# Merged transposing transfers, rows of the summed tanh gradient by DMA, and a shifted last x gradient block in a joint-network training step

## The chip, the cores and the metric

The kernel runs on one core of a Trainium2 chip. The metric is the time of one execution on the device in microseconds (us); a run gives one time, and the median over runs is used. The profile is of one execution, recorded by the hardware profiler.

A core has a matrix engine (PE, with its weight loads in a row of their own, PEld), a vector engine (DVE), an activation engine (ACT), a general engine (POOL) and a sync engine (SP). Each works through its own instructions in order and waits for the others by semaphores. In this kernel SP issues transfers on queue q1 and POOL on queue q0. PE writes into PSUM accumulators, which DVE or ACT copy away.

## The reference

Forward part and gradient of a small joint network: two convolutions with stride 2 over x, a projection, a tanh over the sum of two projections, and an output product.

```python
B, T, D, K, U = 2, 16000, 256, 3, 8
h  = gelu(conv(x, w1))[:, ::2]        # K = 3 taps, 256 -> 256
f  = gelu(conv(h, w2))[:, ::2]        # [2, 4000, 256]
fe = f @ w_f
ge = g @ w_g                          # [2, 8, 256]
j  = tanh(fe[:, :, None, :] + ge[:, None, :, :])
out = j @ w_o                         # [2, 4000, 8, 256]
```

The kernel returns `out` and, for a given `grad_out` of the same shape, the gradients of x, w1, w2, g, w_f, w_g and w_o. All arrays are bfloat16; sums are kept in float32.

## The kernel before

The 4000 output positions of both batch rows are laid one after the other (with 16 columns between) and cut into 16 chunks of 512 columns (`CW`); the last is 336 wide. Features lie on the 128 partitions in two halves (`KT`), positions along the free axis. Products that sum over positions (the weight gradients) need the same data with positions on the partitions ("rows"), so much of the kernel is transposes: by PE through PSUM, or by transposing DMA transfers that SP issues.

The main loop (L829) runs over the chunks n. Within it four steps `up` handle two of the eight u each. A step (`joint_units`, L674) does this for its u: `gj` (L616) squares the tanh JT on ACT into JSQ, multiplies grad_out (GOT, features on partitions) with w_o on PE, and DVE forms NGZ; POOL sums NGZ over u into ACCN and, for the last u, into NGFE (`ngfe_acc`, L636): the summed tanh gradient. Then four blocks of `out` are computed (L694), copied by ACT (L696) and stored by POOL (L721), and the w_o gradient of the step before is accumulated (`gwo`, L725, matmul L733) from JR, the rows of JT, and GO, the rows of grad_out.

Between the units of a step `weave` (L746) sets filler units, 0.92 for each main unit, taken in a written order (`parts`, L833 to L842). For chunk n they are: the first convolution of chunk n+1 (`conv_units`, matmul L320) with the product d1 of chunk n-1 in it (`d1_units`, L424, reading NGFE; DVE writes GF at L426); the row transposes of chunk n-1 braided with the product d5 (`row_units`, `d5_units`, L447); the w_f gradient (`gwf_units`, L506, reading the rows FR of f and NR of NGFE); the w2 gradient (L524); rows of GH; the second convolution of chunk n+1 (L355); and `e_units` (L567): four x gradient blocks (matmul L584, copied by ACT at L587 into GX, stored by POOL at L241) with three w1 gradients (L597) between. After six of the eleven e units stands `fe_units` of chunk n+1 (L379), whose FE feeds the tanh (`tanh`, L390) of the next iteration.

SP issues the transposing transfers: XC, the four phases of x (`load_x`, L164, two chunks ahead, one phase per step); GOT, one per u, two steps ahead (`load_got`, L172); JR, one per u, from JT, a step ahead (`load_jr`, L662); FR, two per chunk (`load_fr`, L469); and the plain transfer GO, one per step (`load_go`, L198). The 512-column tile of 256 features that one of them moves is 256 KB (FR: 128 KB each). NR, the rows of NGFE, is made by PE: eight transposes (L460, in `transposes`) and one DVE copy (L462) at the head of `row_units`.

What sets the order: each tile comes from a pool of so many buffers (`xcp` 6, `gotp` 5, `jtp` 7, `jrp` 2, `frp` 1, `rowp` 6, `gxp` 2), and whoever writes a buffer waits until the last reader of its former content is done. A list scheduler orders the instructions of each engine from the program order and a cost model; the compiled order of each engine is fixed. The transfers issued by SP use eight completion semaphores in turn, so each waits for the eighth before it. The tail after the loop finishes chunk 15.

Of the kernel before, what the change touches and what calls it, by code (L numbers as in the profile page):

```python
# [22 lines left out]
P = 128  # L23
KT = 2
# [8 lines left out]
def kernel(  # L33
# [28 lines left out]
    xq = x.rearrange("b (q four) d -> b four q d", four=4)  # L62
# [39 lines left out]
    xcp = pool("xcp", 6)  # L102
# [10 lines left out]
    rowp = pool("rowp", 6)  # L113
    xrp = pool("xrp", 1)
    gxp = pool("gxp", 2)
    jtp = pool("jtp", 7)
    gotp = pool("gotp", 5)
# [38 lines left out]
    def load_x(n, phases=(0, 1, 3, 2)):  # L156
        W = geom(n)[1]
        for c in phases:
            t = xcp.tile([P, KT, CW + 16], BF16, name="XC")
            back = 16 if c == 3 else 0  # L160
            for lo, hi in gaps(n, back):
                nc.vector.memset(t[:, :, 16 + lo:16 + hi], 0.0)
            for b, q, col, w in segs(n, back):
                nc.sync.dma_start_transpose(out=t[:, :, 16 + col:16 + col + w], in_=xq[b, c, q:q + w, :])  # L164
            S[n]["X", c] = t

    def load_got(n, u):
        t = gotp.tile([P, KT, CW], BF16, name="GOT")
        for lo, hi in gaps(n):
            nc.vector.memset(t[:, :, lo:hi], 0.0)  # L170
        for b, q, col, w in segs(n):
            nc.sync.dma_start_transpose(out=t[:, :, col:col + w], in_=grad_out[b, q:q + w, u, :])  # L172
        S[n]["GOT", u] = t
# [216 lines left out]
    def tanh(n, u):  # L390
        c0, W = geom(n)
        JT = jtp.tile([P, KT, CW], BF16, name="JT")
        S[n]["JT", u] = JT
        for mt in range(KT):
            for b, lo, hi in spans(n):
                nc.scalar.activation(out=JT[:, mt, lo:hi], in_=S[n]["FE"][:, mt, lo:hi], func=ACT.Tanh,  # L396
                                     bias=GE[:, b, mt, u:u + 1], scale=1.0)
        if W % P:
            nc.gpsimd.memset(JT[:, :, W:W // P * P + P], 0.0)

# [62 lines left out]

    def load_fr(n):
        W = geom(n)[1]
        FR = frp.tile([P, KT, 4, P], BF16, name="FR")
        nb = len(blocks(W))
        for kt in range(KT):
            nc.sync.dma_start_transpose(out=FR[:, kt, 0:nb, :], in_=S[n]["FT"][:, kt, 0:nb * P])  # L469
        S[n]["FR"] = FR  # L470

    def row_units(n):
        c0, W = geom(n)
        st = S[n]
        HT, GF, FT, NG = st["HT"], st["GF"], st["FT"], st["NGFE"]
        bl = blocks(W)
        FR = st["FR"]
        t = rowp.tile([P, 8, P], BF16, name="rows")
        st["NR"] = t
        srcs = [(NG[:, kt, o:o + M], 2 * j + kt, M) for j, (o, M) in enumerate(bl) for kt in range(KT)]  # L480
        dsts = [(t[:M, 2 * j:2 * j + 2, :], M, 2 * j, 2 * j + 2) for j, (o, M) in enumerate(bl)]
        if W == CW:
            dsts = [(t[:], P, 0, 8)]
        transposes(srcs, dsts)
        yield
        st["HG"] = []
        s = nsets(n)
        for k, M in sets(n):
            t = rowp.tile([P, 8, P], BF16, name="rows")
            col = lambda off: slice(off + k, off + k + s * (M - 1) + 1, s)  # L490
            srcs = [(HT[:, par, kt, col(2)], 2 * par + kt, M) for par in range(2) for kt in range(KT)]
            srcs += [(GF[:, kt, col(2)], 4 + kt, M) for kt in range(KT)]
            if k == 0:
                srcs += [(HT[:, 1, kt, col(1)], 6 + kt, M) for kt in range(KT)]
            transposes(srcs, [(t[:M, 0:len(srcs)], M, 0, len(srcs))], nc.scalar.copy)
            st["HG"].append(t)
            yield

    def gwf_units(n):
        W = geom(n)[1]  # L500
        FR, t = S[n]["FR"], S[n]["NR"]
        bl = blocks(W)
        ps = ps_f32()
        for k, (o, M) in enumerate(bl):
            for dt in range(KT):
                nc.tensor.matmul(ps[:, dt * D:(dt + 1) * D], lhsT=FR[:M, dt, k, :],  # L506
                                 rhs=t[:M, 2 * k:2 * k + 2, :].rearrange("p k d -> p (k d)"),
                                 start=(k == 0 and dt == 0), stop=(k == len(bl) - 1 and dt == KT - 1))
        flush("F", ACCF[:], ps[:])
        first_flush["F"] = False  # L510
        yield
# [19 lines left out]
    def braid(rows, d5):  # L531
        for gen in (rows, d5, rows, d5, rows, d5, rows, rows, d5):
            yield next(gen, None)
# [118 lines left out]
    def load_jr(n, up):  # L652

        W = geom(n)[1]
        JR = jrp.tile([P, 2, KT, 4, P], BF16, name="JR")
        S[n]["JR", up] = JR
        if n == 0:
            return
        for j in range(2):
            JT = S[n]["JT", 2 * up + j]  # L660
            if W == CW:
                nc.sync.dma_start_transpose(out=JR[:, j].rearrange("p k a d -> p (k a) d"),  # L662
                                            in_=JT[:].rearrange("p k w -> p (k w)"))
            else:
                nb = len(blocks(W))
                for kt in range(KT):
                    nc.sync.dma_start_transpose(out=JR[:, j, kt, 0:nb, :], in_=JT[:, kt, 0:nb * P])
# [99 lines left out]
    idle = xcp.tile([P, KT, CW + 16], BF16, name="XC")  # L767
    nc.vector.memset(idle[:], 0.0)
# [4 lines left out]
    def warm(k):  # L773

        ps = ps_f32()
        for _ in range(k):
            tc.keep_in_program_order(nc.tensor.matmul(ps[:], lhsT=idle[:, 0, 0:P], rhs=idle[:, 0, 0:CW],
                                                      start=True, stop=True))
        yield
# [35 lines left out]
    for i in range(2):  # L815
        load_got(*order[i])
    load_go(*orderp[0])
    for i in range(2, 4):
        load_got(*order[i])
# [7 lines left out]

    for n in range(G):
# [5 lines left out]
        if back:  # L834
            d1, e, rows, ghr = d1_units(n - 1), e_units(n - 1), row_units(n - 1), ghr_units(n - 1)
            parts += [islice(conv, 2), islice(d1, 1), islice(conv, 1), d1, conv, braid(rows, d5_units(n - 1)),
# [3 lines left out]
            parts.append(e)  # L840
# [4 lines left out]
        for up in range(U // 2):  # L845
            step = n * (U // 2) + up
            for i in range(2):
                if 2 * step + 4 + i < len(order):
                    load_got(*order[2 * step + 4 + i])
# [21 lines left out]
            if n + 2 < G:  # L871
                load_x(n + 2, ((0, 1, 3, 2)[up],))
# [5 lines left out]
    for _ in chain(d1_units(n), alternate(row_units(n), d5_units(n)), gwf_units(n), gw2_units(n), ghr_units(n), e_units(n)):  # L878
        pass
# [24 lines left out]
    for b in range(B):  # L904
# [3 lines left out]
        gg_sb = gxp.tile([U, D], BF16, name="gg_sb")  # L908
        nc.scalar.activation(out=gg_sb[:], in_=gg[:U, 0:D], func=ACT.Copy, scale=-1.0)
        nc.sync.dma_start(out=out_4[b], in_=gg_sb[:])  # L910
# [3 lines left out]
        ngR = gxp.tile([U, KT, P], BF16, name="ngR")  # L914
        nc.vector.tensor_copy(out=ngR[:], in_=tr[:U, 0:KT, :])
# [37 lines left out]
```

## Time and profile before

Three runs took 847.09, 842.17 and 854.28 us, a median of 847.09.

| | |
|---|---|
| profiled execution | 845.37 us, its span 843.6 us |
| DVE, ACT, POOL busy | 73%, 81%, 47% |
| mean granted TensorE clock | 0.992 |
| moved by DMA | 187.21 MB, mean 222 GB/s |
| GOT, JR, XC, FR transfers | 136, 128, 68, 32 |
| GO transfers of 512 KB | 56, 5.2 us to landing |
| ACT waits for JR<-JT before a tanh | 8.1 us in 4 waits |

The page gives, for each engine, its busy time and its share of the span; queues with packets, MB and the time that their packets took as a share of sixteen engines' span; and the chain of work that ended last, followed back from the end. A timeline row reads: start, length, engine, line, operation, what it writes and reads, how many in a row, and in brackets the engine's idle time before it with what ended that. A "q" behind an engine's name is its sequencer: a transfer's row on SP is the time that its issue took there, not that of the transfer.

### The profile page before, as it was taken

To read this page: it belongs to the slowest core of one execution; us is meant where nothing else is said; L and a number is where in the kernel's file an instruction comes from. 1 tells how busy PE (TensorE), PEld (TensorE's weight loads), DVE (VectorE), ACT (ScalarE), POOL (GpSimd) and SP (SyncE) were. 2 spreads that over 40 slices of the span, in tenths; PEclk is the share of its full clock that TensorE was granted. 3 is DMA by queue.
4 is the path that set the end of the run, shared out by engine and by line. 5 is a ranking of instruction groups with operands and counts; after the bars stand their busy time and mean duration, and the time that the engine had idled before them with its cause. 6 is when DMAs were issued, how large, how long until landed. Compare 5 with 4: busy or idle time off the path is not lost.

```text
span 843.6 us, 17055 instructions
## 1 busy us (share of the span) xinstructions
PE 816.5 (97%) x6396; PEld 600.8 (71%) x6396; DVE 619.7 (73%) x1217; ACT 679.8 (81%) x1080; POOL 393.8 (47%) x423
## 2 busy tenths in 40 slices
PE   8979999999999999999989999999999999999997
PEld 4556777868777676777757767777776877878796
DVE  4996786877769677696856957769687776967744
ACT  3889997896978969699786886979879697987744
POOL 1145653443544434545465643454444454455661
PEclk9989999999999999999999999999999999999999
DMA  9978999999999999999999999999999999999964
GB/s 197 203 183 182 241 214 235 239 237 219 223 202 230 241 216 265 217 229 212 227 218 220 223 229 212 254 225 253 247 247 220 232 266 242 197 213 223 245 162 135
DMA packets 398515, 187.21 MB, mean 222 GB/s; under 512 B 346464, under 2 KB 382200, under 8 KB 398432
## 3 DMA queue, kind: packets, MB, share of 16 engines
q1 hardware_dynamic: 378112, 119.00, 78.9%
q0 software_dynamic: 20320, 67.12, 27.3%
q8 instruction: 50, 0.82, 0.4%
q14 instruction: 33, 0.27, 0.1%
HBM read 51.38 MB, written 50.34 MB: 121 GB/s over the span
## 4 chain that ended last, share of the span: by engine, by line
PE 71%; ACT 15%; DMA 6%; DVE 6%; issue 2%; ACTq 0%
PE GWO_ps L733 10%; PE ps L694 9%; PE ps L627 8%; PE ps L597 8%; PE ps L584 7%; DMA JR<-JT 6%; PE ps L524 5%; PE ps L320 5%; PE ps L355 4%; PE pst L460 4%; ACT JT L396 4%; PE ps L447 4%; ACT JSQ L621 2%; ACT OUT L696 2%; DVE NGZ L631 2%
## 5 line engine op out<-in xcount | busy, mean ns | idle before, releaser
L631 DVE SCALAR_TENSOR_TENSOR NGZ<-JSQ,ps 128x512 bf16<-128x512 bf16 (+3 forms) x272 | 168.3, 640 | 47.7 <-PE ps L627 44.4
L650 POOL TENSOR_TENSOR ACCN<-ACCN,NGZ 128x1024 f32<-128x1024 f32 (+1 forms) x80 | 168.6, 2107 | 70.8 <-DVE NGZ L631 69.7
L696 ACT CAST OUT<-ps 128x512 bf16<-128x512 f32 (+1 forms) x252 | 148.5, 600 | 53.3 <-PE ps L694 53.1
L396 ACT ACTIVATE JT<-FE,GE 128x512 bf16<-128x512 f32 (+3 forms) x272 | 182.2, 709 | 10.7 <-DMA JR<-JT 8.1
L733 PE MATMUL GWO_ps<-GO,JR 128*128 128x256 bf16 (+1 forms) x1008 | 150.8, 274 | 5.9 <-DMA JR<-JT 3.8
L621 ACT ACTIVATE JSQ<-JT 128x1024 bf16<-128x1024 bf16 (+1 forms) x128 | 135.8, 1064 | 25.5 <-DVE NGZ L631 24.8
L694 PE MATMUL ps<-WO,JT 128*128 128x256 bf16 (+1 forms) x1008 | 149.1, 274 | 2.2 <-ACT rows L462 1.4
L721 POOL DMA_DIRECT2D out_dram<-OUT x76 | 55.8, 734 | 182.8 <-ACT OUT L696 165.4
L627 PE MATMUL ps<-GOT,WOT 128*128 128x512 bf16 (+1 forms) x512 | 138.8, 376 | 1.2 <-ACT OUT L696 1.2
L733 PEld LDWEIGHTS <-JR 128*128 128x128 bf16 (+1 forms) x1008 | 97.0, 98 | 37.0 <-DMA JR<-JT 4.9
L694 PEld LDWEIGHTS <-JT 128*128 128x128 bf16 (+1 forms) x1008 | 98.5, 99 | 25.2 <-issue 4.8
L260 DVE SCALAR_TENSOR_TENSOR g_s<-g_sq,g_x 128x1024 bf16<-128x1024 bf16 (+2 forms) x35 | 65.7, 1876 | 47.8 <-ACT g_sq L260 47.8
L584 PE MATMUL ps<-W1T,GH 128*128 128x256 bf16 (+2 forms) x756 | 100.4, 273 | 0.0
L584 PEld LDWEIGHTS <-GH 128*128 128x128 bf16 (+2 forms) x756 | 83.5, 116 | 13.0
L320 PE MATMUL ps<-XC,W 128*128 128x512 bf16 (+1 forms) x384 | 91.1, 375 | 0.7 <-ACT g_x L323 0.6
L597 PE MATMUL ps<-rows,XR 128*128 128x256 bf16 (+1 forms) x756 | 90.4, 273 | 0.0
L408 DVE TENSOR_TENSOR ACC<-ACC,ps 128x512 f32<-128x512 f32 x90 | 61.5, 684 | 37.6 <-PE ps L524 25.9
L597 PEld LDWEIGHTS <-XR 128*128 128x128 bf16 (+1 forms) x756 | 73.9, 98 | 11.6
L587 ACT CAST GX<-ps 128x512 bf16<-128x512 f32 (+2 forms) x126 | 72.2, 586 | 10.6 <-PE ps L584 4.8
L241 POOL DMA_DIRECT2D out_dram<-GX x67 | 36.7, 548 | 82.2 <-ACT GX L587 77.8
L627 PEld LDWEIGHTS <-WOT 128*128 128x128 bf16 x512 | 48.5, 98 | 33.8 <-issue 2.4
L320 PEld LDWEIGHTS <-W 128*128 128x128 bf16 x384 | 37.4, 98 | 38.2 <-issue 1.0
(132 smaller groups left out, 1230.5 us busy)
## 6 DMA issues: line engine op xcount, KB each, us to landing
GO<-in_grad_out_dram SPq DMA_DIRECT2D x56, 512.0 KB, 5.2
out_dram<-OUT POOLq DMA_DIRECT2D x56, 512.0 KB, 5.8
out_dram<-GX POOLq DMA_DIRECT2D x55, 256.0 KB, 4.5
XR<-in_x_dram POOLq DMA_DIRECT2D x39, 256.0 KB, 6.8
XR<-in_x_dram POOLq DMA_DIRECT2D x13, 320.0 KB, 8.6
GOT<-in_grad_out_dram SPq DMA_TRANSPOSE x136, 5.6
JR<-JT SPq DMA_TRANSPOSE x128, 4.8
GO<-in_grad_out_dram SPq DMA_DIRECT2D x4, 384.0 KB, 5.7
```

Of the source, the lines that this page charges most:

```text
L320: nc.tensor.matmul(ps[:, :W], lhsT=W1[:, i, kt, mt * P:(mt + 1) * P], rhs=st["X", c][:, kt, 16 + sh:16 + sh + W], start=(k == 0), stop=(k ...
L396: nc.scalar.activation(out=JT[:, mt, lo:hi], in_=S[n]["FE"][:, mt, lo:hi], func=ACT.Tanh, bias=GE[:, b, mt, u:u + 1], scale=1.0)
L584: nc.tensor.matmul(ps[:M, cj * D:(cj + 1) * D], lhsT=GH[:, par, kt, o:o + s * (M - 1) + 1:s], rhs=W1T[:, i, kt, :], start=(j == 0), stop=( ...
L587: nc.scalar.copy(out=t[:M, 2 * cp:2 * cp + 2, :], in_=ps[:M, :])
L597: nc.tensor.matmul(ps[:, dt * D:(dt + 1) * D], lhsT=XR[:M, 4 * k + i + 2 * (1 - par), dt * P:(dt + 1) * P], rhs=t[:M, g + 2 * par:g + 2 * ...
L621: nc.scalar.activation(out=JSQ[:, :, :W], in_=JT[:, :, :W], func=ACT.Square)
L627: nc.tensor.matmul(ps[:, :W], lhsT=WOT[:, kt, mt * P:(mt + 1) * P], rhs=GOT[:, kt, :W], start=(kt == 0), stop=(kt == KT - 1))
L631: nc.vector.scalar_tensor_tensor(out=NGZ[:, mt, lo:hi], in0=JSQ[:, mt, lo:hi], scalar=1.0, in1=ps[:, lo:hi], op0=ALU.subtract, op1=ALU.mul ...
L650: st["last"] = nc.gpsimd.tensor_tensor(out=out, in0=in0, in1=st["NGZ", u][:, :, :W], op=ALU.add)
L694: nc.tensor.matmul(ps[:M, j * V:(j + 1) * V], lhsT=st["JT", u][:, kt, o:o + M], rhs=WO[:, kt, :], start=(kt == 0), stop=(kt == KT - 1))
L696: nc.scalar.copy(out=OUT[:M, k, :], in_=ps[:M, :])
L733: nc.tensor.matmul(GWO_ps[:, dt, :], lhsT=JR[:M, j, dt, k, :], rhs=GO[:M, k, j * V:(j + 1) * V], start=(n_gwo[0] == 0), stop=(n_gwo[0] == ...
```

## The change

Five things change.

1. Transposing transfers are merged in pairs. XC holds two phases of x (a phase pair is 512 consecutive values of x in memory), GOT two u, JR two u, FR both halves: one transfer where there were two. The pools become `xcp` 3, `gotp` 3, `jtp` 3 double tiles. Both x pairs of chunk n+2 are loaded in the first two steps of iteration n.
2. NR comes by a transposing transfer (`load_nr`), issued at the start of the iteration ahead of the step's other loads, into a pool of its own with one buffer. Chunk 15, which the tail finishes, still uses PE. `gwf_units` reads the new layout.
3. The last x gradient block of a chunk (the last two of its e units) is left for the next iteration (`rest`), behind the convolution and d1 and ahead of the braid; that of chunk 14 comes at the head of the tail.
4. `braid` alternates without the ninth entry, since `row_units` has a unit less.
5. The tile that the warm-up matmuls read, and two small ones of the end (`gg_sb`, `ngR`), come from the pool `rowp`.

The diff, cut to its core:

```diff
-    xq = x.rearrange("b (q four) d -> b four q d", four=4)
+    xq = x.rearrange("b (q c two) d -> b c q (two d)", c=2, two=2)
...
-    xcp = pool("xcp", 6)
+    xcp = pool("xcp", 3)
...
+    nrp = pool("nrp", 1)
...
-    jtp = pool("jtp", 7)
-    gotp = pool("gotp", 5)
+    jtp = pool("jtp", 3)
+    gotp = pool("gotp", 3)
...
-    def load_x(n, phases=(0, 1, 3, 2)):
+    def load_x(n, pairs=(0, 1)):
         W = geom(n)[1]
-        for c in phases:
-            t = xcp.tile([P, KT, CW + 16], BF16, name="XC")
-            back = 16 if c == 3 else 0
+        for c in pairs:
+            t = xcp.tile([P, 2, KT, CW + 16], BF16, name="XC")
+            back = 16 * c
...
             for b, q, col, w in segs(n, back):
-                nc.sync.dma_start_transpose(out=t[:, :, 16 + col:16 + col + w], in_=xq[b, c, q:q + w, :])
-            S[n]["X", c] = t
+                nc.sync.dma_start_transpose(out=t[:, :, :, 16 + col:16 + col + w].rearrange("p c k w -> p (c k) w"),
+                                            in_=xq[b, c, q:q + w, :])
+            for j in range(2):
+                S[n]["X", 2 * c + j] = t[:, j]
...
-            nc.sync.dma_start_transpose(out=t[:, :, col:col + w], in_=grad_out[b, q:q + w, u, :])
+            nc.sync.dma_start_transpose(out=t[:, :, :, col:col + w].rearrange("p u k w -> p (u k) w"),
+                                        in_=grad_out[b, q:q + w, 2 * up:2 * up + 2, :].rearrange("q u v -> q (u v)"))
...
+    def load_rows(pool_, name, src, W):
+        t = pool_.tile([P, KT, 4, P], BF16, name=name)
+        if W == CW:
+            nc.sync.dma_start_transpose(out=t[:].rearrange("p k a d -> p (k a) d"), in_=src.rearrange("p k w -> p (k w)"))
...
+    def load_nr(n):
+        S[n]["NR"] = load_rows(nrp, "NR", S[n]["NGFE"][:], geom(n)[1])
...
+        if W == CW:
+            nc.sync.dma_start_transpose(out=JR[:].rearrange("p u k a d -> p (u k a) d"),
+                                        in_=S[n]["JTP", up][:].rearrange("p u k w -> p (u k w)"))
+            return
...
-            parts += [islice(conv, 2), islice(d1, 1), islice(conv, 1), d1, conv, braid(rows, d5_units(n - 1)),
+            parts += [islice(conv, 2), islice(d1, 1), islice(conv, 1), d1, conv, rest, braid(rows, d5_units(n - 1)),
...
-            parts.append(e)
+            parts.append(islice(e, 3))
+            rest = e
...
+            if back and up == 0:
+                load_nr(n - 1)
+            if step + 2 < len(orderp):
+                load_got(*orderp[step + 2])
...
-                load_x(n + 2, ((0, 1, 3, 2)[up],))
+                load_x(n + 2, ((0,), (1,), (), ())[up])
...
-    for _ in chain(d1_units(n), alternate(row_units(n), d5_units(n)), gwf_units(n), gw2_units(n), ghr_units(n), e_units(n)):
+    for _ in chain(rest, d1_units(n), alternate(row_units(n), d5_units(n)), gwf_units(n), gw2_units(n), ghr_units(n), e_units(n)):
```

## The prediction, made before the changed kernel ran

> **What bounds the kernel now.** I read the page first (busy times, queues), then the chain of waits over the whole run, then the timelines of SP, PE, POOL and ACT over one iteration.
>
> ```profile
> PE 816.5 (97%) x6396; PEld 600.8 (71%) x6396; DVE 619.7 (73%) x1217; ACT 679.8 (81%) x1080; POOL 393.8 (47%) x423
> q1 hardware_dynamic: 378112, 119.00, 78.9%
> q0 software_dynamic: 20320, 67.12, 27.3%
> ```
>
> PE is the bound (97%). q1 carries what SP issues; its packets and q0's add up to 106% of the engines' span, so the DMA engines are seldom empty.
>
> ```profile
> 136.97 1.03 PE ps L447 x4
> 187.21 1.03 PE ps L447 x4
> 237.46 1.03 PE ps L447 x4
> 261.55 7.14 DMA JR<-JT
> 281.29 4.81 DMA JR<-JT
> 290.63 1.03 PE ps L447 x4
> 340.88 1.03 PE ps L447 x4
> 391.40 1.00 PE ps L447 x4
> ...
> 501.17 1.03 PE ps L447 x4
> 552.67 1.03 PE ps L447 x4
> 602.93 1.03 PE ps L447 x4
> ```
>
> The same point of each iteration in the chain of waits. From 136.97 to 237.46 an iteration takes 50.25 us, and again from 290.63 to 340.88 and from 552.67 to 602.93. Between them some are longer: 53.2 to 290.63, 109.8 for the two to 501.17, 51.5 to 552.67. The first such mark is at 86.72, the last at 703.43: twelve iterations in 616.7 us, and 12 x 50.25 = 603.0, so 13.7 us are stalls. In the long ones the chain runs through JR<-JT, a transfer. Why is it late?
>
> ```profile
> 221.49 4.39 SPq L662 DMA_TRANSPOSE JR<-JT  x2
> ...
> 230.69 5.15 SPq L164 DMA_TRANSPOSE XC<-in_x_dram  x1
> 235.94 3.18 SPq L172 DMA_TRANSPOSE GOT<-in_grad_out_dram  x1
> 239.21 10.87 SPq L164 DMA_TRANSPOSE XC<-in_x_dram  x5
> 250.18 2.62 SPq L662 DMA_TRANSPOSE JR<-JT  x2
> ```
>
> In SP's timeline one issue follows the other with 0.1 us between. The JR pair issued at 250.18 reads JT that ACT had finished by 217.8 (the tanh rows behind FE at 208.84, counted), and PE wants it about 254.7: SP's queue is some 32 us behind and the margin is gone.
>
> **The change part by part.** From the timelines of PE and POOL, and from the view of single tiles (least, median and longest issue in ns):
>
> ```profile
> 229.44 0.61 PE L460 MATMUL pst<-ident,NGFE 128*128 128x128 bf16 x8
> 229.88 0.60 PE L694 MATMUL ps<-WO,JT 128*128 128x256 bf16 x4
> 217.62 2.44 POOL L650 TENSOR_TENSOR NGFE<-ACCN,NGZ 128x1024 bf16<-128x1024 f32 x1 [1.04 <-DVE NGZ L631]
> L662 SPq DMA_TRANSPOSE JR<-JT x112: 1232/1405/4122, 69.5 to 775.4; - x112
> L469 SPq DMA_TRANSPOSE FR<-FT x32: 1177/1257/2328, 29.0 to 803.8; - x32
> ```
>
> NR by DMA. Eight PE transposes leave each iteration: from 229.44 to the next row at 229.88 is 0.44 us, on a PE that never waits there. Chunks 0 to 14 take the transfer, chunk 15 keeps PE: 15 x 0.44 = 6.6 us off the path. The DVE copy (688 ns) leaves too; DVE is at 73% and I count nothing. In its place SP issues one transpose of 256 KB. It waits for NGFE, which POOL ends at 217.62 + 2.44 = 220.06. Its reader (L506, the w_f gradient) starts at 238.76. Issued at 220.1 and landing after JR's median 4.8 us it is there at 225, after JR's longest, 13.5 us, at 233.6: hidden either way. Were SP still 15 us behind, PE would wait for it. Queued behind NR on SP are JR of the next step, GO and GOT. That JR was issued at 221.49 before and is wanted at 239.6, so waiting for 220.06 costs it nothing; all else behind it is wanted later. The single NR buffer is free since the previous chunk's L506, thirty us earlier. On q1, 256 KB cost 0.262 / 119.00 x 78.9% of 843.6 us = 1.5 us of packet time, 22 us over the run: hidden only if q1 has that room (rival 2).
>
> Double transfers. Per iteration 8 GOT, 8 JR, 4 XC and 2 FR become 4, 4, 2 and 1; with NR that is 12 in place of 22, while the 4 GO stay. No row shows an issue of 512 KB. From below: the issue is a fixed cost, since 128 KB (FR) takes at least 1177 ns and 256 KB (JR) 1232, so 512 KB would take about 1.34. From above: twice a 256 KB issue, 2.46 at the least, and all that the queue adds on top doubles with the bytes. By the medians (GOT 1.73, JR 1.41, XC 1.70, FR 1.26, GO 0.57, 0.09 between) SP spends 39 us per iteration before, nearer 47 with the long ones that the medians hide; after it, 22 by the lower price and 40 by the upper. I take 30, nearer the lower, because FR and JR stand closest to what is asked and differ by 5% at twice the bytes. Ends for the stalls: all 13.7 us go, or none; I take 11, four fifths. If JR is in time, the next to be late would be GOT, whose landing now waits for 512 KB: the narrowest GOT before was issued by 423.7 and wanted at 428.8, at the time when SP was furthest behind.
>
> [...]
>
> Buffers. XC 6 single to 3 double: the same bytes, and the second pair waits for the end of the convolution (229.0), as the last phase did. GOT 5 to 6 tiles: a step's GOT no longer waits for the step's own first u. JT 7 to 6: a tanh waits for JR three steps back; ACT waited 8.1 us for that in all, in 4 waits, only where JR was late. I count nothing; the ends are -1 and +8 us, and those 8 belong to late JRs.
>
> The last x gradient block. Its 12 matmuls (1.31 us by the chain's L584 rows), two ACT casts (586 ns each) and POOL's store move behind the convolution of the next iteration. PE's sum is the same; chunk 14's block falls into the tail. It stands between the GF product (DVE, done at 230.06) and its reader (L447, 230.32) where the 0.44 us of transposes stood, so a small wait of 0.2 us there may go. POOL is idle from 230.3 to 234.5, where the store falls. ACT, however, has no gap from 208 to 240 (rival 3). Counted at nothing, ends -0.2 and +1.2 us an iteration.
>
> Start and end. Two XC transfers replace four; the first convolution needs all of x in place of three phases, at 9.44 us, when the fourth had just landed (9.3). The other moved tiles (warm-up, gg, ngR) are off the path. Zero, ends -1 and +1.
>
> **Sum.** The profiled execution took 845.37 us: span 843.6 and 1.8 around it; the median of the runs shown, 847.09, is 1.7 above it. 843.6 - 6.6 - 11.0 = 826.0, plus 1.8: 828 us.
>
> **Rivals.**
>
> 1. The doubled transfers take twice as long, and the queue stays late. q1's 78.9% and the 106% speak for it, FR against JR speaks against. Only the transposes go: 843.6 - 6.6 + 1.8 = 839 us.
>
> 2. Slower: q1 becomes the bound. If bytes set SP's pace, NR's transfer comes on top. From 237.46 to 552.67 the late stretch ran at 315.2 / 6 = 52.5 us an iteration; with 1.5 us more it is 54.0, while PE needs 49.8. Eight such iterations in place of the stalls seen: 8 x (54.0 - 50.25) = 30 against 13.7, so 845.4 + 16, and PE's saving is lost in the wait: about 862 us, less or more by an iteration or two. It decides as soon as q1's work per iteration exceeds 49.8 us. For it: SP has no gap in the stretch. Against: from 552.67 to 703.43 the same work ran at 50.25 without a stall, and q1 has 21% of the span without packets.
>
> 3. ACT gives back what the queue gains. Two casts more in the stretch without gaps, 1.17 us in 14 iterations, hold up the accumulators that PE needs: 828 + 16 = 844 us. For it: ACT is solid from 208 to 240. Against: the casts come out of the same stretch (216 to 218), so its sum is as before.
>
> **How the numbers follow.** Forecast 0.57, rival 1 0.22, rival 2 0.13, rival 3 0.08. About 2% is what a measurement of this kernel can tell from no change: 830 and 864 us against 847. The forecast's own range is 820 to 836 (all stalls and the small waits gone; stalls of 10 us left); some three quarters of it lie under 830, so faster 0.44. Slower takes most of rival 2 and a little for what I have not seen: 0.12. Same 0.44. The range, 819 to 848, holds the forecast, rivals 1 and 3, and leaves out rival 2 and mishaps.
>
> **What the profile after would show.** Right: the L447 marks 49.8 us apart nearly throughout; no JR<-JT in the chain; NGFE gone from L460's rows; double issues of about 1.3 us where the queue is empty; SP with gaps, waiting for NGFE before NR. Rival 1: double issues of 2.5 us and more, back to back, and JR still in the chain. Rival 2: marks over 52 us apart. Rival 3: PE waiting on ACT between the convolution and L506. My forecast would be wrong if a double transfer costs more than two single ones, or if another engine's wait, now covered by late JRs, takes their place.

## The result and the profile after

The changed kernel takes 890.75 us, the median of six runs (887.26 to 901.49), against 847.77 for the kernel before in the same measurement. The ratio is 1.055, with a 95% interval of 1.050 to 1.060: it is slower by 43 us, and the prediction of 828 us, with a range to 848, is wrong. The profiled execution took 901.49 us (span 899.7), 11 us over the median, so I use its parts and not its sum.

The head of the page after, then its chain by engine:

```profile
PE 818.8 (91%) x6276; PEld 594.9 (66%) x6276; DVE 633.4 (70%) x1196; ACT 683.9 (76%) x1080; POOL 402.6 (45%) x423
q1 hardware_dynamic: 388896, 123.03, 78.6%
PE 45%; ACT 21%; DVE 19%; DMA 9%; issue 5%; SPq 1%; POOL 0%; DVEq 0%; ACTq 0%; POOLq 0%
```

PE has 120 transposes fewer (x6276 against x6396), but its busy time hasn't fallen (818.8 against 816.5 us), and 6% of the span more than before are idle. q1 moved 4.03 MB more in the same share of time. No engine became the bound: less than half of the chain is PE, and ACT, DVE and a transfer share the rest.

The chain of waits: an early stretch, by L360, the second convolution, and a later one by the d5 matmuls, now L453:

```profile
135.11 14.54 DMA JR<-JT
...
216.15 1.30 PE ps L360 x6
...
241.24 9.84 DMA JR<-JT
...
276.08 1.30 PE ps L360 x6
...
589.04 1.03 PE ps L453 x4
...
641.42 1.03 PE ps L453 x4
```

Two things are seen. Where the kernel runs evenly, an iteration now takes 52.38 us (641.42 - 589.04, and the same twice more up to 746.18), against 50.25 before and 49.8 in my forecast, with no transfer in the chain. I call such an iteration an even one. And early in the run JR is late for longer than it ever was: from 216.15 to 276.08 are 59.9 us.

The issues on SP, from the view of single tiles (least, median and longest in ns; JR 512 KB, FR 256 KB):

```profile
L676 SPq DMA_TRANSPOSE JR<-JT x56: 1484/4052/6051, 74.8 to 819.5; - x56
L473 SPq DMA_TRANSPOSE FR<-FT x15: 1232/1250/5171, 30.2 to 803.2; - x15
```

The least issue of JR, 1.48 us, is near that of half its size (1.23); the median is 4.05, where two single ones had taken 2 x 1.41. For FR the merging did what I had hoped: 1.25 us for 256 KB, as before for 128.

The late JR, row by row, in the timelines of SP, ACT and PE:

```profile
135.11 5.04 SPq L676 DMA_TRANSPOSE JR<-JT  x1
149.67 0.72 ACT L402 ACTIVATE JT<-FE,GE 128x512 bf16<-128x512 f32 x1 [12.16 <-DMA JR<-JT]
151.35 0.58 PE L466 MATMUL pst<-ident,HT 128*128 128x128 bf16 x4 [13.19 <-ACT rows L468]
```

JR is issued right behind NR (129.54, whose issue took 5.40 us). A tanh on ACT waits 12.16 us until JR has read the pair of tanh tiles that it wants to write. The copy of rows stands behind that tanh on ACT and starts at 150.30, and PE, whose accumulators ACT would have emptied, stands for 13.19 us. It then pays a second time. In the view by stretches (from:to, length, then busy time of PE, PEld, DVE, ACT, POOL, the granted clock, DMA):

```profile
141.00:151.30 10.30, 0.00 (x0) 0.00 (x0) 0.00 (x0) 1.63 (x3) 0.99 (x2) 0.54 1.22 210
151.30:155.40 4.10, 4.05 (x17) 2.11 (x17) 1.20 (x2) 4.10 (x6) 0.00 (x0) 0.50 0.87 196
```

Over the first 4.1 us after the wait the granted clock is 0.50, after that 1.00: by these numbers about another 2 us are lost.

The even iterations show three short waits of PE, all for ACT. They are (PE had written the two accumulators of GX from 629.65 to 630.47 and from 630.74 to 631.56):

```profile
634.26 0.57 ACT L603 CAST GX<-ps 128x512 bf16<-128x512 f32 x1
634.88 1.08 PE L643 MATMUL ps<-GOT,WOT 128*128 128x512 bf16 x4 [0.79 <-ACT GX L603]
637.86 0.38 PE L466 MATMUL pst<-ident,HT 128*128 128x128 bf16 x4 [0.93 <-ACT rows L468]
641.42 1.03 PE L453 MATMUL ps<-GF,W2T 128*128 128x512 bf16 x4 [0.56 <-ACT rows L468]
```

GX is emptied 3.6 to 3.8 us after PE is done with it, because its two casts stand in ACT's line, and the rows behind them come late as well. These are the two casts that the change moved here. So there were two theories when the experiments began: A, the pairs of tanh tiles make ACT, and through it PE, wait for JR; B, the shifted x gradient block costs time in every iteration. A third, C, came up with the first results: the transfer of NR makes JR late.

### The profile page after: what moved, and what is told of

Read it like the earlier page. It is cut to its first block, busy times and chain, and to the rows that moved or that the text cites. A ratio compares the mean times of both kernels' runs of the same rounds, so it can differ in the third digit from the quotient of the medians.

```text
span 899.7 us, 16502 instructions
## 1 busy us (share of the span) xinstructions
PE 818.8 (91%) x6276; PEld 594.9 (66%) x6276; DVE 633.4 (70%) x1196; ACT 683.9 (76%) x1080; POOL 402.6 (45%) x423
## 4 chain that ended last, share of the span: by engine, by line
PE 45%; ACT 21%; DVE 19%; DMA 9%; issue 5%; SPq 1%; POOL 0%; DVEq 0%; ACTq 0%; POOLq 0%
DMA JR<-JT 9%; DVE g_sq L273 7%; PE ps L613 6%; PE ps L600 6%; PE GWO_ps L748 6%; DVE NGZ L647 5%; PE ps L709 5%; PE ps L540 5%; ACT JT L402 4%; PE ps L360 4%; PE ps L643 4%; ACT JSQ L637 3%; ACT rows L468 3%; ACT g_s L265 3%; ACT OUT L711 3%
## 5 line engine op out<-in xcount | busy, mean ns | idle before, releaser
L402 ACT ACTIVATE JT<-FE,GE 128x512 bf16<-128x512 f32 (+3 forms) x272 | 179.3, 700 | 35.6 <-DMA JR<-JT 35.2
L666 POOL TENSOR_TENSOR ACCN<-ACCN,NGZ 128x1024 f32<-128x1024 f32 (+1 forms) x80 | 170.6, 2132 | 78.3 <-DVE NGZ L647 77.4
L647 DVE SCALAR_TENSOR_TENSOR NGZ<-JSQ,ps 128x512 bf16<-128x512 bf16 (+3 forms) x272 | 165.5, 639 | 35.0 <-PE ps L643 33.1
L637 ACT ACTIVATE JSQ<-JT 128x1024 bf16<-128x1024 bf16 (+1 forms) x128 | 133.7, 1050 | 46.2 <-DVE NGZ L647 46.1
L600 PE MATMUL ps<-W1T,GH 128*128 128x256 bf16 (+2 forms) x756 | 102.5, 273 | 0.0
L325 PE MATMUL ps<-XC,W 128*128 128x512 bf16 (+1 forms) x384 | 93.9, 383 | 0.6 <-ACT g_x L328 0.6
L613 PEld LDWEIGHTS <-XR 128*128 128x128 bf16 (+1 forms) x756 | 74.0, 98 | 11.5
```

The lines of the kernel that those rows point to most:

```text
L325: nc.tensor.matmul(ps[:, :W], lhsT=W1[:, i, kt, mt * P:(mt + 1) * P], rhs=st["X", c][:, kt, 16 + sh:16 + sh + W], start=(k == 0), stop=(k ...
L600: nc.tensor.matmul(ps[:M, cj * D:(cj + 1) * D], lhsT=GH[:, par, kt, o:o + s * (M - 1) + 1:s], rhs=W1T[:, i, kt, :], start=(j == 0), stop=( ...
L613: nc.tensor.matmul(ps[:, dt * D:(dt + 1) * D], lhsT=XR[:M, 4 * k + i + 2 * (1 - par), dt * P:(dt + 1) * P], rhs=t[:M, g + 2 * par:g + 2 * ...
L637: nc.scalar.activation(out=JSQ[:, :, :W], in_=JT[:, :, :W], func=ACT.Square)
L647: nc.vector.scalar_tensor_tensor(out=NGZ[:, mt, lo:hi], in0=JSQ[:, mt, lo:hi], scalar=1.0, in1=ps[:, lo:hi], op0=ALU.subtract, op1=ALU.mul ...
L666: st["last"] = nc.gpsimd.tensor_tensor(out=out, in0=in0, in1=st["NGZ", u][:, :, :W], op=ALU.add)
```

## The experiments

All ratios are to the kernel before, run on the same chip beside each kernel; medians of kernels from different measurements are compared by these ratios only. For each iteration I give the time from one first d5 matmul to the next; where lines of another row are shown, they are as far apart. "Iterations 7 to 9" are those whose chunks lie around the border of the two batch rows, where transfers come in two pieces; in the kernel before they take 53.84, 53.79 and 53.69 us. The last iteration of the loop takes 35.25 us there.

**e1: no shift.** The change, with the x gradient block back in its iteration.

```diff
-            parts.append(islice(e, 3))
-            rest = e
+            parts.append(e)
```

> The changed kernel with its last x gradient block back in its own iteration; everything else of the change stays. Theory B (the shift puts two more GX casts into ACT's solid stretch, and the new order lets VectorE's gelu run beside GpSimd's additions, so that PE waits three times in each iteration): the steady iteration falls from 52.38 us to 50.3 or less, twelve to fourteen times, and the kernel to 855 to 867 us; the long stalls in iterations 2, 3 and the last stay. Theory A (a pair of tanh tiles is given back only when a whole JR of 512 KB has landed, ACT stands in line behind that, PE behind ACT): almost all of the loss is in the long stalls, which this edit does not touch: 880 to 895 us, with gaps of 6 to 13 us left. If both hold, this run shows the first number and e3 the other.

Measured: 857.07 us, ratio 1.018 (1.009 to 1.027). The even iteration is 49.33 us, 3.05 less than in the changed kernel:

```profile
244.29 1.03 PE ps L360 x4
293.61 1.03 PE ps L360 x4
```

PE, which stood for 0.79, 0.93 and 0.56 us in the changed kernel's even iteration, has no wait in that of e1. The long stalls in iterations 2 and 3 (65.43 and 61.64 us) are gone too, though both theories had them stay; one of 8.7 us before the tail stays. So theory B holds as to the place, for 3.6% of the kernel, and what is left of the loss, 1.8%, lies elsewhere. One half of theory B falls: VectorE's gelu runs beside GpSimd's additions in e1 as well (2.51 us at 269.15, an addition from 268.66 to 271.11), and VectorE is busy for longer in e1's even iteration (39.9 us) than in the changed kernel's (38.6). How much of the 3.6% the early stalls are in a median execution is not known: beside them, one early iteration takes 57.34 us in e3 and 58.25 in g1, and none is stalled in g2, all three with the shift.

**f1: the shift alone**, on the kernel before (the same lines added).

> The kernel before with the last x gradient block in the next iteration and nothing else. Theory B: 868 to 885 us, the steady iteration up by 2 to 2.8 us from 50.25, with PE waiting for ACT's GX and rows. Theory A: within 1% of the kernel before, 840 to 855 us, since tanh tiles and transfers are as they were.

Measured: 865.03 us, ratio 1.028 (1.014 to 1.041). The even iteration is 51.74 us against 50.25:

```profile
251.39 1.30 PE ps L355 x6
303.13 1.30 PE ps L355 x6
```

1.5 us in each even iteration without any of the rest; theory B again. Together with the other parts of the change the shift costs twice that (3.05); which of them doubles it was not tested.

**e3: six single tanh tiles** in the memory of the three pairs, and with them two single JR transfers for each pair again (the diff is cut to the tiles).

```diff
-    jtp = pool("jtp", 3)
+    jtp = pool("jtp", 6)
...
-        if u % 2 == 0:
-            S[n]["JTP", u // 2] = jtp.tile([P, 2, KT, CW], BF16, name="JT")
-        S[n]["JT", u] = JT = S[n]["JTP", u // 2][:, u % 2]
+        S[n]["JT", u] = JT = jtp.tile([P, KT, CW], BF16, name="JT")
```

> The changed kernel with the tanh tiles as six single buffers in the memory of its three pairs, so JR comes as two transfers of 256 KB again and each gives back one tile; everything else of the change stays. Theory A (pairs of tanh tiles): ACT's waits of tanh on JR fall from 35.2 us to below 12, the iterations of 65.43 and 61.65 us to about 53, and the kernel to 858 to 870 us. Theory B (the shift): the 52.38 us iterations stay as they are, and if the stalls come from SP's queue and not from the tiles' size, they stay too: 880 to 895 us. Six tiles are one less than the kernel before had, so some of the stalls can stay under theory A as well.

Measured: 883.74 us, ratio 1.049 (1.038 to 1.059), not clearly below the changed kernel. The wait that theory A is about did shrink, from 35.2 us in 8 waits:

```profile
ACT JT L400 <- DMA JR<-JT: 9.5, 4, 4.9
```

but the even iterations stay at 52.38. By the ratios theory A is worth 0.6%, some 5 us of the 43, and the two intervals overlap, so it is not clear of noise.

**f3: merging alone**, on the kernel before: all double transfers with their buffers (and the moved small tiles), rows of the tanh gradient by PE, no shift.

> The kernel before with the double transfers and their pair buffers alone (x, output gradient, JR, FR); rows of the tanh gradient by PE and the last x gradient block as before. Theory A (pairs of tanh tiles): the long stalls come with the pairs, 868 to 885 us, the steady iteration 50.3 us. Theory B (the shift): no loss is here; with the queue relieved, 833 to 847 us. A third theory (the transfer for the rows of the tanh gradient, 256 KB ahead of JR on the same queue, makes JR late): 833 to 847 us here too, and this run is told from theory B by e1, which keeps that transfer.

Measured: 842.09 us, ratio 1.003 (0.998 to 1.007): no difference. By the profile (span 841.0) gains and losses cancel. The even iteration is 49.77 us, 0.48 less; iterations 7 to 9 take 50.57, 51.85 and 49.77, together 9.1 us less. But the first d5 comes at 82.56 us instead of 79.65, and the last iteration of the loop takes 43.83 us instead of 35.25, with this in it:

```profile
786.97 1.04 ACT L401 ACTIVATE JT<-FE,GE 128x336 bf16<-128x336 f32 x2 [8.71 <-DMA JR<-JT]
788.74 1.01 PE L706 MATMUL ps<-WO,JT 128*128 128x256 bf16 x4 [7.15 <-ACT rows L467]
```

Theory A's price of 25 us or more is not there. With e1 it shows what NR by DMA costs: 1.5%, though it takes another 0.44 us off each even iteration.

Where f3's gains come from, the timelines of PE show in part. In iterations 7 to 9 its waits of 0.15 us and more fall from 8.3 to 2.2 us, and the three of GWO for JR (0.84, 1.34 and 0.85 us) are gone. In the even iteration of the kernel before, PE is held up twice at the end of the braid, by 0.27 us for ACT's rows and by 0.21 us behind that (the rows at 236.81 and 237.46); in f3 both are gone.

**f4: merging without the tanh tiles**: f3 with seven single tiles and single JR transfers.

> The kernel before with double transfers for x, the output gradient and FR, while the tanh tiles stay seven single buffers and JR two transfers; rows of the tanh gradient by PE, no shift. f3, which has the pairs too, had steady iterations of 49.77 us and lost 8 us in the iteration before the last (43.83 us against 35.25, with a gap of 7.41 us behind a tanh that waits 8.71 us for JR). Theory A (three pairs give a tile back later than seven singles): that gap goes and the iteration falls to 35 to 37 us, so the kernel comes to 829 to 836 us. Rival: the gap belongs to the queue or to the last chunk's four transfers for each JR, and stays: 838 to 846 us. If the gain in the steady iterations came from the merged JR, they go back to 50.25 us and the kernel to 840 or more.

Measured: 847.95 us, ratio 1.010 (1.007 to 1.013). Theory A was wrong about the last iteration: it takes 43.87 us, with seven single tiles.

```profile
771.19 1.34 SPq L174 DMA_TRANSPOSE GOT<-in_grad_out_dram  x1
788.79 0.57 ACT L399 ACTIVATE JT<-FE,GE 128x336 bf16<-128x336 f32 x1 [8.33 <-DMA JR<-JT]
```

The pair of GOT of the short last chunk, issued at 771.19, lands at 782.29, and JR, issued right behind it from 774.84 on, at 788.7. The even iterations are back at 50.26, with the two short waits of the kernel before, so some 0.5 us an iteration come with the merged JR and its pairs of tanh tiles.

**f5: merging alone, last chunk mended.** f3, with two GOT transfers for each pair of the short chunk.

```diff
+            if geom(n)[1] < CW:
+                for j in range(2):
+                    nc.sync.dma_start_transpose(out=t[:, j, :, col:col + w], in_=grad_out[b, q:q + w, 2 * up + j, :])
+            else:
```

> f3 (all double transfers, neither the transfer for the rows of the tanh gradient nor the shift) with one thing undone: the output gradient of the last, short chunk (336 rows instead of 512) comes as two transfers for each pair again, into the same pair of buffers. Theory D (in f4 such a pair transfer took 11.1 us from issue to landing, and JR, which stands behind it, came 8 us late for the tanh that waits for its tile): the gap of 7.4 us in the last iteration but one goes, that iteration falls from 43.83 us to 35 to 38, and the kernel to 832 to 838 us, 0.5 to 1.5% below the kernel before. Rival (the gap is of the stores and input reads that run there beside every transfer, or of the pairs of tanh tiles): the iteration stays at 42 us or more, and the kernel at 839 to 846 us.

Measured: 837.40 us, ratio 0.998 (0.994 to 1.002). The last iteration takes 35.47 us, and ACT's longest wait for JR in the whole kernel is now 3.6 us; theory D holds. Why the double transfer of 336 rows takes so long was not asked. It is the fastest kernel of this study, but not faster than the one before by more than the measurement can tell.

**f8: f5 with two small loads first.**

```diff
+    nc.gpsimd.dma_start(out=GR8[:], in_=g.rearrange("b u d -> u b d"))
+    nc.gpsimd.dma_start(out=WG[:], in_=w_g.rearrange("(kt p) n -> p kt n", p=P))
     nc.gpsimd.dma_start(out=W1[:], in_=w1.rearrange("i (kt p) n -> p i kt n", p=P))
```

> f5 with the two small loads that the first matmuls wait for (GR8 and WG) issued ahead of the load of W1 on GpSimd's queue, nothing else. In the kernels with the double x transfers the first d5 of the program came at 81 to 83 us (83.28 in f5) against 79.65 in the kernel before, with waits of 1.3 to 3.3 us for these loads at 9 to 11 us. Theory G (the double x transfers run beside the small loads and hold them up): the first d5 comes at 79 to 80 us and the kernel at 831 to 836 us, 0.6 to 1% below the kernel before. Rival (the loads arrive when they did, since the transfers share the same engines, or W1 is late instead): 82 us or more, and 836 to 842 us.

Measured: 842.62 us, ratio 1.003 (0.997 to 1.008); the first d5 at 84.32 us, later still. Theory G falls, and the loads came out as the rival had it: GR8 is there in time, but PE waits 3.02 us for WG and 0.61 for W1. So the order of these loads is no cure, and why the start is 1 to 5 us longer in most kernels with double x transfers (not in f4: 79.62) stays open. Its last iteration takes 39.20 us, so theory D's gain of 8.4 in f5 is not sure in every execution.

**f2 and f7: NR on and off, single tanh tiles.** Both are the kernel before with double transfers for x and FR only; f2 has NR by DMA as well.

> The kernel before with the rows of the tanh gradient by one transfer first in the iteration and double transfers for x and FR; output gradient and tanh tiles stay single (five and seven buffers); no shift. The rows off PE are worth 0.44 us in each of 14 iterations (e1 has steady iterations of 49.33 us against 49.77 in f3). Theory C (the transfer of 256 KB ahead of JR uses up the room on the queue that the merging made, which shows where the chunk is broken in two, iterations 7 to 9, 54.4 to 54.8 us in e1 against 49.8 to 51.9 in f3): 848 to 862 us with iterations 7 to 9 above 53 us. Rival (e1's loss there was the pairs, not the transfer): iterations 7 to 9 at 50 to 52 us, the last but one at 35 to 37, and 826 to 836 us.

> f2 without the transfer for the rows of the tanh gradient: the kernel before with double transfers for x and FR alone; output gradient and tanh tiles single, rows by PE, no shift. Theory C (that transfer of 256 KB, issued ahead of JR, is what made JR late for PE's GWO in f2, 13.0 us in 6 waits, and lengthened five of its iterations to 51.7 to 60.6 us): no such wait above 4 us in all, all full iterations at 49.7 to 52 us, and 833 to 845 us. Rival (single transfers of JR and the output gradient are enough to fill the queue): iterations 7 to 9 stay at 53.7 us or more as in the kernel before, and the kernel at 842 to 856 us.

Measured: f2 from 852.49 to 874.00 us in four executions, too far apart for a ratio, so I use its waits only, from an execution of 868.79 us; f7 850.96 us, ratio 1.016 (1.007 to 1.025). PE's wait for JR in GWO, us in all, times, longest, in f2 and then in f7:

```profile
PE GWO_ps L745 <- DMA JR<-JT: 13.0, 6, 3.4
```

```profile
PE GWO_ps L742 <- DMA JR<-JT: 1.4, 2, 1.1
```

As to the waits this is what theory C said: with NR PE waits for JR, without it hardly, with single tanh tiles as with pairs. Its other signs are missed: f7's iterations 7 to 9 take 50.91, 54.57 and 51.74 us, 4 us less than before, but one is over the 52 named, and the time, above that of the kernel before, lies where the rival had it. Merging x and FR alone is no gain.

**c1: NR by DMA on f5**, the cleanest test of that part: e1 with the short chunk's GOT single.

> f5 (all double transfers, the last chunk's output gradient single, no shift) plus the transfer for the rows of the tanh gradient: the two differ in this one part. Theory C (that transfer, issued ahead of JR, uses up what the merging freed on the queue, above all in iterations 7 to 9, where the chunk is broken in two): 0.44 us won in each of the other iterations and more lost in these, 843 to 855 us against 837.4 for f5. Rival (with the last chunk mended, nothing is left against that transfer): 14 x 0.44 = 6 us below f5, 828 to 834 us, which would also beat the kernel before.

Measured: 855.37 us, ratio 1.020 (1.010 to 1.030), 2.2% above f5. Two of its iterations do take 49.33 us. Five take 50.05 to 50.10, more than f5's 49.77, with two waits of PE for ACT's rows (0.31 and 0.14 us). The rest give back more: 59.70 us in iteration 7, where SP needed 16.9 us to issue two x transfers and JR stood behind them, issued at 408.64:

```profile
391.65 16.88 SPq L165 DMA_TRANSPOSE XC<-in_x_dram  x2
```

In its view of waits:

```profile
ACT JT L406 <- DMA JR<-JT: 21.4, 9, 7.6
```

f5 has 13.5 us in 7 waits there, the longest 3.6. The last iteration takes 42.49 us, where f5 had 35.47. So the price of NR by DMA is shown; that it comes from NR's place ahead of JR is argued, since no kernel issued NR behind JR.

**Why does the shift cost that much?** Four kernels ask this. g1 empties the shifted block's accumulators by VectorE; g2 puts the block behind the w2 gradient; g3 puts it first in the next iteration; f6 is f1 with a third buffer for the squares (and the two small tiles of the end in `rowp`, as in the change). The diff is that of g1.

```diff
-                nc.scalar.copy(out=t[:M, 2 * cp:2 * cp + 2, :], in_=ps[:M, :])
+                (nc.vector.tensor_copy if k == bl[-1][0] else nc.scalar.copy)(out=t[:M, 2 * cp:2 * cp + 2, :], in_=ps[:M, :])
```

> The changed kernel, shift and all, with the two accumulators of the shifted x gradient block emptied by VectorE instead of ACT. Theory B1 (the price of the shift is ACT's two more casts of 1.17 us in a stretch where ACT has no idle time): the steady iteration falls from 52.38 to 49.5 to 50.6 us and the kernel to 850 to 868 us. Theory B2 (the price lies in PE's order: with the block at that place PE asks for accumulators faster than ACT and VectorE together give them back): VectorE is as full there, the iteration stays at 51.7 to 52.6 us and the kernel at 875 to 895 us.

> The changed kernel with the shifted block later in the next iteration, behind the weight gradients of the second convolution instead of ahead of the braid of rows and d5. Theory B1 (ACT's solid stretch under the braid, where each of the rows' accumulators is emptied by ACT too, is what can't take the two casts): the block now lies beside units that VectorE empties, the steady iteration falls to 49.3 to 50.5 us and the kernel to 850 to 868 us. Theory B2 (any place in the next iteration costs the same, since ACT and the accumulators are as full everywhere): 52 us and 875 to 895 us stay.

> The changed kernel with the shifted block as the first work of the next iteration's fill, ahead of conv, instead of ahead of the braid: it is still taken past the iteration's boundary, but lies nearest to where it was. Theory B1+B2 (the stretch of conv's casts, the gelu and the rows is what can't take two more accumulators for ACT): the block is out of that stretch, the steady iteration falls from 52.38 us to 49.3 to 50.3, and the kernel to 852 to 868 us. Theory F (what hurts is that the block no longer runs at the end of the iteration): 51.5 us or more and 875 to 893 us.

> f1 (the shift alone on the kernel before) with a third buffer for the squares JSQ. In all kernels with the shift ACT waits longer for VectorE's NGZ before it may write the next square: 69.5 us in 40 waits in f1 against 24.8 us in 14 in the kernel before. Theory E (the shift's price is ACT standing in line behind these waits, so that rows and GX are emptied late): the wait goes, the steady iteration falls from 51.73 to 50.3 to 50.8 us, and the kernel from 865 to 846 to 856 us. Theory B2 (the price is the order in which PE asks for accumulators, and ACT waits because it has nothing else to do): the iteration stays at 51.3 us or more, the kernel at 858 to 870 us.

Measured:

| | us | ratio | even iteration, us |
|---|---|---|---|
| the change | 890.75 | 1.055 (1.050 to 1.060) | 52.38 |
| g1, by VectorE | 884.77 | 1.055 (1.049 to 1.062) | 51.41 |
| g2, later | 874.40 | 1.047 (1.038 to 1.056) | 51.68 |
| g3, first | 882.35 | 1.050 (1.036 to 1.064) | 51.60 |
| f6, to f1's 51.74 | 866.47 | 1.034 (1.028 to 1.040) | 53.17 |
| e1, no shift | 857.07 | 1.018 (1.009 to 1.027) | 49.33 |

None of them brought the gain that it tried for. ACT's two casts are worth 0.97 us of the 3.05 in the even iteration, which g1's time doesn't show, and another place 0.7 or 0.8; g3's 51.60 us is what theory F had asked. The third buffer makes the even iteration longer, but it took only 10 of the 69.5 us of ACT's waits for NGZ, so theory E is not refuted by it; nothing here supports it. What remains was asked by leaving the block out, which leaves a part of the x gradient uncomputed:

```diff
-            parts.append(islice(e, 3))
-            rest = e
+            parts.append(islice(e, 3) if fwd else e)
```

> The changed kernel with the shifted block left out in all chunks but the last one's (its twelve matmuls, two casts and its store; so a part of the x gradient is not computed). PE's share of the block is 12 x 0.109 = 1.31 us. Theory B1+B2 (the block is too much where it was put): without it the steady iteration is what e1 has less that share, 49.33 - 1.31 = 48.0 us, and the kernel 830 to 845 us. Theory F (the block is missed where it was taken from, at the end of the iteration, where its matmuls covered the way from the last NGZ over the summed gradient and GF to the first rows): PE waits there also without it, 48.8 us or more in each iteration, and 845 to 865 us.

Measured: 850.37 us, ratio 1.014 (1.000 to 1.027). The even iteration, with 1.31 us of matmuls and 1.17 us of casts less than e1, takes as long as e1's 49.33:

```profile
247.86 1.30 PE ps L360 x6
297.16 1.30 PE ps L360 x6
```

Theory F holds. In its old place the block cost next to nothing: while PE worked on it, ACT and VectorE came through with what the braid of rows and d5, and the products behind it, need next. Without it PE is there earlier and waits:

```profile
281.94 0.25 PE L466 MATMUL pst<-ident,GF 128*128 128x128 bf16 x1 [0.32 <-DVE XC L163]
285.89 1.02 PE L643 MATMUL ps<-GOT,WOT 128*128 128x512 bf16 x4 [0.31 <-ACT rows L468]
```

In the two other iterations that I read, the first of these waits is put down to VectorE's GF. A third, at the w2 gradient, is 0.14 us, for ACT's rows. Measured from row to row against e1, PE loses 0.49, 0.47 and 0.31 us at these places, 1.27 in all, nearly the 1.31 that it had saved. g2, where the block is gone from its old place too, has the same two waits for rows (0.31 and 0.14) and one of 1.26 us for GF.

Put in front of the braid, the block costs 52.38 - 49.30 = 3.08 us, more than its matmuls and its casts together. 1.31 of it are its own matmuls, which no wait hides any more; most of the other 1.77 is in PE's waits, which rise from 0.8 to 2.3 us and are now all for ACT. Not settled is which of the waits of ACT and VectorE makes up how much: g1 names 0.97 as ACT's casts, and no run separates the rest. The whole kernel is less clear than its even iteration: the ratios of x1 and e1, 1.014 and 1.018, are no different within their intervals.

## Why the prediction was wrong

**The shift: the step that failed most.** I wrote "Counted at nothing, ends -0.2 and +1.2 us an iteration", on the ground that PE's sum and ACT's sum stay the same. ACT's nearly does: it is busy for 42.8 us of an even iteration, and 42.5 in e1. But the same sum in another place is not the same time: x1 shows that the block was free where it stood, in the even iterations, and these show that it costs 3.05 us where it was put (1.5 us on the kernel before). By the medians, 890.75 against e1, it is 1.055 / 1.018, 3.6% or about 31 us of the 43. I had the rows to see a part of it: ACT solid from 208 to 240. Rival 3, which I gave 0.08 and 16 us, names that part, the two casts (0.97 us an iteration by g1); against it I held that the casts come out of the same stretch. They came out of its beginning and went to its middle, and a sum over 32 us hides that. The larger part, that PE's 1.31 us had been covering a wait, is in none of my rivals.

**NR by DMA: the gain was right, the cover was not.** 0.44 us an iteration is what e1 shows against f3 (49.77 to 49.33). c1 has it in two iterations only. That NR's transfer costs nothing, since "all else behind it is wanted later", was wrong. I checked JR's margin in the one iteration where I had looked at the queue; in c1 JR is late around the border of the batch rows (a wait of 5.34 us in iteration 7) and in the last iteration (7.59). Price, from f3 to e1 and from f5 to c1: 1.5 and 2.2%, 13 to 18 us, net of what NR gains. Rival 2 named this exchange, but as a bound of bytes. The even iterations of e1, at 49.33 with NR's bytes, say that it is not that; the loss lies in some of the others.

**Double transfers: right where I looked, zero in sum.** I took 11 us of 13.7 in stalls as gained. f3 gains 9.1 us in iterations 7 to 9 and 0.48 in each even one, and loses 8.6 in the last iteration and 2.9 at the start. The term for start and end, "Zero, ends -1 and +1", is the mis-sized one: +11.5 in f3. The short chunk's transfers never came up in my working. The price of an issue failed with it. "I take 30, nearer the lower": by the medians of the changed kernel SP spends 4 x 4.05 (JR) + 4 x 4.29 (GOT) + 2 x 3.09 (x) + 2 x 1.25 (FR, NR) + 4 x 0.58 (GO), and 0.09 between each, about 46 us an iteration, above my upper end of 40 and above the 39 of the same sum before. Its rows added up over one even iteration say it better, since the medians hide the long ones: SP issued for about 47.5 us both before (180.07 to 230.32) and in f5 (233.0 to 282.76). Fewer issues took as long. The first double x transfer did take 1.42 us, near my lower price. In f5, where little is late, JR's median is still 3.13 us; in the changed kernel it is 4.05, beside a landing of 6.5, where one single issue before took 1.41 beside a landing of 4.8. So what merging gained did not come from a shorter queue on SP as I had put it. The waits that are gone in f3 are named above; why JR and the rows come earlier there, no run shows.

**Buffers.** "I count nothing" for three pairs instead of seven tiles; ACT's waits for JR went from 8.1 to 35.2 us. By e3 that is worth some 5 us, within the end of +8 that I gave and not clear of noise; the waits are long only beside NR and the shift (f3, with pairs and without those, waits 14.2 us).

**What was right.** The transposes left PE, no engine became the bound by bytes, and the two signs that I named for rival 3 and rival 1 are in the trace: PE waiting for ACT between the convolution and the w_f gradient, and double issues of 2.5 us and more with JR in the chain. Rival 1 had the merging at nothing, as f3 has it, but there by luck: its reason, a queue that stays late, would have kept the stalls of iterations 7 to 9, and these did shrink, while others came.

## What to carry to other kernels

Before a piece of work is moved to another place, leave it out and time the rest: if the time doesn't fall, it was filling a wait, and moving it opens that wait again and adds the work to another stretch. Judge a transfer put ahead of others by the iteration with the least margin, which was here where chunks are broken or short, not by an even one. And three small edits made together can hide from one another: merging alone changes nothing here that the measurement can tell, and the other two cost 13 to 18 us and 23 to 31 us.

## What the runs showed of the hardware

Some of VectorE's operations take longer beside GpSimd's additions. In the changed kernel's timeline, the summation over u and VectorE's gelu beside it:

```profile
619.74 2.19 POOL L666 TENSOR_TENSOR NGFE<-ACCN,NGZ 128x1024 bf16<-128x1024 f32 x1 [1.63 <-issue]
619.98 2.50 DVE L273 TENSOR_TENSOR g_sq<-g_sq,g_x 128x1024 bf16<-128x1024 bf16 x1
```

This VectorE operation takes 0.69 us elsewhere; here it begins 0.24 us after an addition and ends 0.55 us after it. Another, of 0.42 us elsewhere, took 2.29 at 616.11, beside an addition from 615.97 of 2.14. Which operation it is differs from kernel to kernel. In the kernel before one takes 2.50 us at 218.11, beside the addition from 217.62 to 220.06, and in e1 one 2.51 at 269.15; both end 0.55 us after the addition, too. For f1 and f3 I have the means alone: an operation of 0.69 us is at 1.10 over 39 times in f1, another at 1.53 over 26 times in f3. VectorE's NGZ, which reads one of its inputs from PSUM, keeps its 0.68 us beside an addition (600.30, in an addition from 599.93 of 2.13) as elsewhere.

In the changed kernel the granted clock falls to half for multiples of 3.41 us around PE's longer waits: from 141.80 to 155.45, four times 3.41, of which PE had work in the last 4.1; from 251.03 on for 6.82, with a wait of 5.78 up to 253.90; and from 841.53 on for 10.24, with one of 9.16 up to 847.11. All changes of the clock in that trace lie whole multiples of 3.41 us apart. It fell around some shorter waits as well: in both kernels PE waits 2.1 us for VectorE ahead of a GWO row (up to 58.45 before, up to 61.27 after), and the clock stands at half from 58.58 for 6.83 us and from 63.29 for 3.42. In the 3.4 us ahead of that PE was busy for 1.29 and 1.05. Around the changed kernel's waits of 2.02 us (up to 463.89) and 2.40 (up to 794.53) it stayed at 1.00. What tells these waits apart, no run shows.

An issue on SP has no fixed price here: 1.42 us for the first double x transfer of the changed kernel, 4.68 for the second, issued right behind it, and 16.88 for two of them in c1. What held the longer ones up was not shown.
